# One of five w_gate rows per partition moved to the head of ScalarE's DMA queue, with x behind it

## The chip, the cores and the metric

The kernel runs on one core of one Trainium2 chip. A core has five engines with an instruction queue each: PE (TensorE), DVE (VectorE), ACT (ScalarE), POOL (GpSimd) and SP (SyncE). Transfers between DRAM and on-chip memory are issued from an engine's queue, here from SP and ACT, and carried by 16 DMA engines that all queues share. The metric is the device time of one execution in microseconds (us); less is better.

## What is computed

One decode step for a batch of two tokens with 640 features: layer norm, attention with 32 heads of 192 over the last 2048 positions of a cache of 8192, its output projection and a residual, then layer norm again, a gated feed-forward network of width 1536 and a second residual. Everything stored is bf16.

```
h  = x + A(layernorm(x))                       # x [2, 1, 640]
#    q = xn @ wq [640, 6144]; k, v = the last 2048 of 8192 positions, 32 heads x 192
#    p = softmax(q k^T * 192**-0.5);  A = (p v) @ wo [6144, 640]
n  = layernorm(h)
h2 = h + (gelu(n @ w_gate) * (n @ w_up)) @ w_down   # w_gate, w_up [640, 1536]; w_down [1536, 640]
```

## The kernel before

The work is a single stream of weights and cache through one on-chip buffer, `ring`, of six slots of 24,576 bytes per partition. The 32 heads and two tokens make 16 groups (`NG`), each with one K load and one V load of 3072 KB (24,576 bytes in each of 128 partitions). wq takes 7680 KB, wo comes in four loads of 1920 KB, w_gate is one load of 1920 KB, w_up has two pieces and w_down four (`WUC`, `WDC`, lines 218 and 219). `load` (line 331) puts a transfer on a list, `pump` (line 334) issues it from SP as soon as the loads that lay at its place in the ring were used (`done`, line 349). So all of these go through SP's queue in the order of lines 411 to 422: K0, wq, K1, V0, K2, V1 and so on, then wo, w_gate, w_up, w_down. SP issues a load many microseconds before its bytes move, because earlier loads are still queued.

The one load that SP does not issue is x: line 410 issues it from ACT's queue, ahead of everything else on that engine (line 441, a table load, is next). x is two rows of 1280 bytes. PE's first work is to turn x (`_x_T`, line 466); a layer norm (`layernorm`, line 446) that goes back and forth between DVE, PE and ACT makes xnT from it. Behind the layer norm, in program order on DVE, come the constants (lines 477 to 521), and behind these the copies of K's transposes out of PSUM (line 567).

For each group PE transposes K (`transposes`, line 543), then come scores, softmax, the exponentials' columns and the products with V (`pv`, line 651). `q_rows` (line 569) needs xnT and wq; once it has run, wq's part of the ring is free and SP may issue K2.

The end of the kernel is a chain: `pv(15)`, `o_rows(3)`, `oproj(2)`, `o_columns(3)`, `oproj(3)` (line 696, needs the last wo load), the mean and `h_columns`, hnT (line 779), the w_gate matmuls, the gate's activation, the w_up matmuls, and `uT`, the product of both. The w_down matmuls (line 850) follow in four pieces as their loads land, then one copy (line 856) and the store of the result (line 857).

`ffn_in` (line 792) issues the matmuls of w_gate or w_up. A partition p holds the five rows 5p to 5p+4 of the weight (index c); each c gives four matmuls (line 801) that add into one PSUM bank. Its argument `parts` says which c go together, `loads` which of them came with which load; the instructions of a part wait for hnT and for the load of that part. For w_gate the call is cut in two so that `row_scale` (line 785), the row's normalisation, can go between.

`_Prog` (line 51) keeps the order in which operations are written for each engine, and finds from the names of what they read and write (R, W, X) which semaphores each has to wait for.

Of the kernel before, what the change touches and what calls it, by code (L numbers as in the profile page):

```python
# [5 lines left out]
BF16 = mybir.dt.bfloat16  # L6
# [8 lines left out]
NC5 = D // 128  # L15
# [4 lines left out]
F = 1536  # L20
# [200 lines left out]
K_AT = (0, SLOT, 3 * SLOT, 5 * SLOT)  # L221
# [6 lines left out]
def bass_sequential_preLN__sliding_block_cached__geglu_ffn__decode_kernel(  # L228
# [12 lines left out]
    with ExitStack() as ctx:  # L241

        def sb(name, shape, dt):
            return ctx.enter_context(nc.sbuf_tensor(name, shape, dt))

        def ps(name, shape, dt):
            return ctx.enter_context(nc.psum_tensor(name, shape, dt))
# [29 lines left out]
        ge = sb("ge", [128, 6, 5], F32)  # L277

        xrow = sb("xrow", [128, D], BF16)
        xT = sb("xT", [128, NC5, B], F32)  # L280
        ls = sb("ls", [128, 2, B], F32)
        dT = sb("dT", [128, 2, NC5, B], F32)
# [38 lines left out]
        sps = ps("sps", [128, 512], F32)  # L321
# [4 lines left out]
        P = _Prog()  # L326


        where, live, queue, used = {}, [], [], set()

        def load(key, off, nbytes, src, shape, sem):
            queue.append((key, off, nbytes, src, shape, sem))
# [24 lines left out]
        def load_k(g):  # L357
            load(("k", g), K_AT[g % 4], SLOT, kv_src(A_k_cache, g), lambda v: v, f"k{g % 4}")
# [14 lines left out]
        def wo_parts(J):  # L373
            return ((0, 12),)

        def load_ffn():
            load(("wg", 0), K_AT[1], 2 * NC5 * F, B_w_gate.rearrange("(p c) f -> p c f", c=NC5),
                 lambda v: v.rearrange("p (c f) -> p c f", f=F), "wg")
            for i, (c0, c1) in enumerate(WUC):
                load(("wu", i), K_AT[3] + 2 * c0 * F, 2 * (c1 - c0) * F, B_w_up.rearrange("(p c) f -> p c f", c=NC5)[:, c0:c1, :],  # L380
                     lambda v: v.rearrange("p (c f) -> p c f", f=F), f"wu{i}")
            wd = B_w_down.rearrange("(q p s) n -> q p s n", p=128, s=6)
            for i, (f0, f1) in enumerate(WDC):
                q = f0 // 6
                load(("wd", i), WD_AT[i], 2 * (f1 - f0) * D, wd[q][:, f0 - 6 * q:f1 - 6 * q, :],
                     lambda v: v.rearrange("p (s n) -> p s n", n=D), f"wd{i}")


        def dve(fn, R=(), W=(), X=(), cls=1):
            return P.op("dve", fn, R, W, X, cls=cls)  # L390
# [4 lines left out]
        def pe(fn, R=(), W=(), X=()):  # L395
            return P.op("pe", fn, R, W, X)
# [4 lines left out]
        def ts(out, in0, s1, op0, s2=None, op1=None):  # L401
            def fn(e):
                kw_ = {"op1": op1} if op1 is not None else {}
                return e.tensor_scalar(out=out, in0=in0, scalar1=s1, scalar2=s2, op0=op0, **kw_)  # L404
            return fn

        def tt(out, a, b, op):
            return lambda e: e.tensor_tensor(out=out, in0=a, in1=b, op=op)  # L408

        P.op("act", lambda e: e.dma_start(xrow[0:2, :], A_x[:, 0, :]), W=["xrow"], dma="dx")  # L410
        load_k(0)
        load_wq()
# [7 lines left out]
        load_wo(2)  # L420
        load_wo(3)
        load_ffn()
        pump()

# [360 lines left out]
        def row_scale():  # L785
            pe(lambda e: e.matmul(tps[2][0:98, 0:1], lhsT=lsx[:, :, :].rearrange("p r x -> p (r x)")[:, 0:98], rhs=onesd[:, 0:1],  # L786
                                  start=True, stop=True), R=["lsx", "onesd"], X=[("t", 2)])
            act(lambda e: e.activation(out=lnv[0:98, :], in_=tps[2][0:98, 0:1], func=ACT.Ln, bias=eps_t[0:98, :], scale=1.0),  # L788
                R=["eps"], W=["lnv"], X=[("t", 2)])
            act(lambda e: e.activation(out=rstd[0:98, :], in_=lnv[0:98, :], func=ACT.Exp, scale=-0.5), R=["lnv"], W=["rstd"])  # L790

        def ffn_in(bank, xt, key, parts, loads):
            for c0, c1 in parts:
                i = max(k for k, q in enumerate(loads) if q[0] <= c0)
                wv, wtoks = where[key, i]

                def fn(e, c0=c0, c1=c1, wv=wv, l0=loads[i][0]):
                    for c in range(c0, c1):
                        for r in range(4):
                            cols = wv[:, c - l0, 768 * (r // 2):768 * (r // 2 + 1)].rearrange("p (x s) -> p x s", s=6)  # L800
                            ins = e.matmul(bank[32 * r:32 * r + 2, 0:384], lhsT=hnT[:, c, :], rhs=cols[:, :, 3 * (r % 2):3 * (r % 2) + 3],
                                           start=(c == 0), stop=(c == NC5 - 1), tile_position=(0, 32 * r))
                    return ins

                pe(fn, R=["hnT"] + wtoks, X=[xt])
# [16 lines left out]
        def rjb(t):  # L822
            return t.rearrange("p (r j b) -> p r j b", r=4, j=3)

        ffn_in(sps, "s", "wg", ((0, 2),), ((0, NC5),))
        row_scale()
        ffn_in(sps, "s", "wg", ((2, NC5),), ((0, NC5),))
        dve(ts(grow[0:98, 0:384], sps[0:98, 0:384], rstd[0:98, 0:1], ALU.mult), R=["rstd"], W=["sm"], X=["s"])
        pe(h_rows, R=["hrow", ("hsel", 0), ("hsel", 1)], X=["m1"])
        gT = ffn_columns(grow, ["sm"], tps[0], 0)  # L830
# [10 lines left out]
            W=[("osb", 0), ("osb", 1)], X=["o"])  # L841
        vT = ffn_columns(urow, [("osb", 0), ("osb", 1)], tps[1], 1)
        dve(tt(uT[:, :, 0:17:16].rearrange("p (r j) b -> p r j b", r=4), vT, rjb(ga[:, 0, :]), ALU.mult), R=["ga0"], W=["uT"], X=[("t", 1)])
        for i, (f0, f1) in enumerate(WDC):
            wd, wtoks = where["wd", i]

            def fn(e, f0=f0, f1=f1, wd=wd):
# [10 lines left out]
             dma="dout")  # L858
# [43 lines left out]
```

## Time and profile before

| what | value |
|---|---|
| median of 3 runs | 293.38 us (293.36 to 293.39) |
| the profiled execution | 293.39 us |
| its span, first to last instruction | 291.9 us |
| outside the span | 1.49 us |
| mean granted TensorE clock | 0.842 |
| PE, DVE, ACT busy | 67%, 44%, 33% of the span |
| moved by DMA | 122.44 MB, 419 GB/s over the span |
| w_gate, issue to landing | 1920 KB, 32.4 us |
| a K load, a V load, issue to landing | 31.8 us, 27.7 us (medians) |

Busy shares are averages over stages with different limits. A busy PE need not be what the time hangs on; the chain of waits, followed back from the last instruction, says what was waited for. "PEld" is PE's weight load, "SPq" and "ACTq" stand for the issuing of a transfer in those engines' queues. In the line of 40 slices each digit is a busy share in tenths. Times in the timeline are in us from the start of the span: start, duration, engine, line, what is written from what, how many, and in brackets how long the engine was idle before and what ended that.

### The profile page before, as it was taken

Reading aid. Unit: us, or ns where it says so; the run is one execution under the profiler, and the core shown is the slowest. Engines: PE = TensorE matmul, PEld = TensorE weight load, DVE = VectorE, ACT = ScalarE, POOL = GpSimd, SP = SyncE. Lnnn points to the kernel's source line nnn. Section 1 sums busy time; section 2 is a strip of 40 time slices with the busy share of each in tenths; the row PEclk is TensorE's granted clock in tenths of the full one; section 3 lists DMA queues with packets and bytes.
Section 4 is the critical chain, followed back from the end, with each engine's and each line's share of the span. In section 5 each row is a group of like instructions: output and inputs, shape, how many; then the busy total and the mean of one; then the engine's idle time right before and its main releaser. Section 6 shows DMA issues by size and latency. Waiting matters only on the chain.

```text
span 291.9 us, 5055 instructions
## 1 busy us (share of the span) xinstructions
PE 195.0 (67%) x2141; PEld 151.1 (52%) x2141; DVE 128.4 (44%) x311; ACT 96.1 (33%) x120; POOL 8.6 (3%) x36
## 2 busy tenths in 40 slices
PE   2450768858579197849494597658596858585784
PEld 1450445837376184629282585456575656553341
DVE  5950085434336263616264155426267426262231
ACT  2150125533333152616152154325254325251001
POOL 4000020000000000000000000000000000000000
PEclk9995799797959689977988599979689979796557
DMA  7998999999999999999999999999999999999994
GB/s 290 428 498 362 433 431 430 434 430 431 427 416 445 428 431 429 431 431 431 431 411 442 431 431 428 431 431 428 431 428 428 431 431 428 431 431 426 425 414 174
DMA packets 6362, 122.44 MB, mean 419 GB/s; under 512 B 718, under 2 KB 848, under 8 KB 1360
## 3 DMA queue, kind: packets, MB, share of 16 engines
q1 hardware_dynamic: 6348, 122.30, 98.1%
q8 instruction: 7, 0.11, 0.2%
q14 instruction: 3, 0.02, 0.0%
q10 hardware_dynamic: 4, 0.00, 0.0%
HBM read 122.29 MB, written 0.00 MB: 419 GB/s over the span
## 4 chain that ended last, share of the span: by engine, by line
DMA 76%; PE 19%; SPq 2%; DVE 1%; ACT 1%; issue 0%
DMA ring<-in_A_k_cache_dram 57%; PE tps L555 15%; DMA ring<-in_A_wq_dram 10%; DMA ring<-in_B_w_down_dram 10%; SPq L347 2%; PE tps L576 2%; PE ops L657 1%; ACT ktr L564 1%; PE m L708 1%; PE m L690 1%; DVE ering L408 0%; PE m L850 0%; DVE ktr L567 0%; PE m L641 0%; PE m L671 0%
## 5 line engine op out<-in xcount | busy, mean ns | idle before, releaser
L555 PE MATMUL tps<-identf,ring 128*128 128x128 f32 x768 | 114.4, 317 | 47.6 <-DMA ring<-in_A_k_cache_dram 46.6
L555 PEld LDWEIGHTS tps<-identf,ring 128*128 128x128 f32 x768 | 105.7, 166 | 50.9 <-DMA ring<-in_A_k_cache_dram 48.0
L564 ACT ACTIVATE ktr<-tps 128x1024 bf16<-128x1024 bf16 x80 | 79.3, 1023 | 86.3 <-PE tps L555 86.2
L567 DVE COPY ktr<-tps 128x1024 bf16<-128x1024 bf16 x112 | 74.2, 688 | 74.3 <-PE tps L555 73.6
L632 ACT ACTIVATE eexp<-sm,nm 128x512 bf16<-128x512 f32 x16 | 11.5, 721 | 63.0 <-DVE nm L630 63.0
L657 PE MATMUL ops<-ring,ering 128*32 128x384 bf16 x512 | 25.0, 339 | 3.5 <-DMA ring<-in_A_v_cache_dram 3.4
L621 DVE CUSTOM_DVE_ANT_1 sm<-sps,mska 128x512 f32<-128x512 f32 x16 | 11.1, 691 | 33.7 <-PE sps L613 33.7
L613 PE MATMUL sps<-ktr,rq 128*16 128x512 bf16 x384 | 24.6, 389 | 1.1 <-POOL rq L408 1.1
L657 PEld LDWEIGHTS ops<-ring,ering 128*32 128x32 bf16 x512 | 12.7, 99 | 12.3 <-DMA ring<-in_A_v_cache_dram 5.4
L613 PEld LDWEIGHTS sps<-ktr,rq 128*16 128x16 bf16 x384 | 9.3, 88 | 11.3 <-POOL rq L408 1.2
L628 PEld LDWEIGHTS m<-mrhs,pm 128*128 128x128 bf16 x16 | 1.5, 96 | 23.4 <-DVE mrhs L404 23.4
L628 PE MATMUL m<-mrhs,pm 128*128 128x16 bf16 x16 | 2.9, 183 | 15.7 <-DVE mrhs L404 15.7
L576 PE MATMUL tps<-ring,xnT 128*32 128x384 bf16 x80 | 4.8, 412 | 10.8 <-DMA ring<-in_A_wq_dram 10.8
L408 POOL TENSOR_TENSOR rq<-qs,mask 128x96 bf16<-128x96 bf16 x16 | 5.6, 359 | 194.6 <-PE sps L613 161.5
L576 PEld LDWEIGHTS tps<-ring,xnT 128*32 128x32 bf16 x80 | 2.7, 119 | 12.7 <-issue 11.0
L599 DVE CAST qs<-ops 128x384 bf16<-128x384 f32 x1 | 0.6, 558 | 16.6 <-PE ops L594 16.6
L408 DVE TENSOR_TENSOR ering<-m,mask 128x256 bf16<-128x256 f32 x16 | 6.7, 418 | 2.4 <-PE m L641 2.3
L708 PE MATMUL m<-ring,ot 128*2 128x320 bf16 x96 | 5.5, 382 | 1.6 <-DMA ring<-in_A_wo_dram 1.6
L788 ACT ACTIVATE lnv<-tps,eps_t 98x1 f32<-98x1 f32 x1 | 0.3, 261 | 17.2 <-PE tps L786 17.2
L583 ACT ACTIVATE qrow<-tps 128x768 bf16<-128x768 f32 x1 | 0.8, 810 | 14.6 <-PE tps L576 14.6
L641 PE MATMUL m<-sel,eexp 128*128 128x64 bf16 x64 | 4.8, 200 | 1.2 <-ACT eexp L632 1.2
L408 DVE TENSOR_TENSOR orow<-m,wm 128x1536 bf16<-128x1536 f32 x3 | 5.3, 1751 | 0.0
(124 smaller groups left out, 88.1 us busy)
## 6 DMA issues: line engine op xcount, KB each, us to landing
ring<-in_A_k_cache_dram SPq DMA_DIRECT2D x16, 3072.0 KB, 31.8
ring<-in_A_v_cache_dram SPq DMA_DIRECT2D x16, 3072.0 KB, 27.7
ring<-in_A_wq_dram SPq DMA_DIRECT2D x1, 7680.0 KB, 28.2
ring<-in_A_wo_dram SPq DMA_DIRECT2D x4, 1920.0 KB, 21.8
ring<-in_B_w_gate_dram SPq DMA_DIRECT2D x1, 1920.0 KB, 32.4
ring<-in_B_w_up_dram SPq DMA_DIRECT2D x1, 1536.0 KB, 24.7
ring<-in_B_w_down_dram SPq DMA_DIRECT2D x1, 960.0 KB, 27.2
ring<-in_B_w_down_dram SPq DMA_DIRECT2D x1, 480.0 KB, 27.9
```

Of the source, the lines that this page charges most:

```text
L347: P.op("sp", lambda e, v=v, src=src: e.dma_start(v, src), W=toks + [("sem", sem)], dma=sem)
L408: return lambda e: e.tensor_tensor(out=out, in0=a, in1=b, op=op)
L555: ins = e.transpose(tps[bi][:, 128 * u:128 * (u + 1)], kv[:, off:off + 128], identf[:, :])
L564: act(lambda e, dst=dst, bv=bv: e.activation(out=dst, in_=bv, func=ACT.Copy), W=[("kt", n)], X=[("t", bi)])
L567: dve(lambda e, dst=dst, bv=bv: e.tensor_copy(dst, bv), W=[("kt", n)], X=[("t", bi)], cls=0)
L576: ins = e.matmul(tps[0][32 * r:32 * (r + 1), 0:384], lhsT=xnT[:, c, 32 * J:32 * (J + 1)], rhs=wq[:, c, 1536 * J + 384 * r:1536 * J + 384 * ...
L613: ins = e.matmul(sps[32 * ch:32 * ch + 16, :], lhsT=rq[:, g % 4, k, :], rhs=ktr[:, k // 2, 1024 * ch + k % 2:1024 * (ch + 1):2], start=(k ...
L621: dve(lambda e: e.tensor_tensor_reduce(out=sm[:, :].rearrange("p (u x) -> p u x", u=4), in0=sps[:, :].rearrange("p (u x) -> p u x", u=4), ...
L632: act(lambda e: e.activation(out=eexp[:, :], in_=sm[:, :], func=ACT.Exp, bias=nm[:, 0:1], scale=1.0, accum_out=zr[:, g % 4:g % 4 + 1]), R= ...
L641: ins = e.matmul(o, lhsT=eexp[:, 128 * u:128 * (u + 1)], rhs=sel64[:, :], start=True, stop=True)
L657: ins = e.matmul(ops_[32 * r:32 * (r + 1), 0:384], lhsT=ering[:, g % 4, t, :], rhs=vv[:, 384 * t:384 * (t + 1)], start=(g % 4 == 0 and t < 4),
L708: ins = e.matmul(m1[32 * r:32 * r + 2, 192:512], lhsT=ot[:, kk, :], rhs=wo[:, kk - k0, 320 * h:320 * (h + 1)], start=(kk == 1 or J < 2 and ...
```

## The change

A buffer `wgh` of 3072 bytes per partition is added. A new function `load_wg0` loads row c = 0 of w_gate's five into it, 384 KB in 128 pieces of 3072 bytes, from ACT's queue; it is called before the line that loads x, so x is now the second entry of that queue. The load of w_gate in the ring keeps its place in SP's order and its start in the ring, and carries the other four rows, 1536 KB in pieces of 12,288 bytes where there were 1920 KB in pieces of 15,360. The calls of `ffn_in` for w_gate name two loads; the first call has two parts where it had one. The matmuls and their order are the same.

```
+        wgh = sb("wgh", [128, 1, F], BF16)
...
+        def load_wg0():
+            where["wg", 0] = wgh[:, :, :], ["wgh"]
+            P.op("act", lambda e: e.dma_start(wgh[:, 0, :], B_w_gate.rearrange("(p c) f -> p c f", c=NC5)[:, 0, :]), W=["wgh"], dma="wg0")
+
         def load_ffn():
-            load(("wg", 0), K_AT[1], 2 * NC5 * F, B_w_gate.rearrange("(p c) f -> p c f", c=NC5),
-                 lambda v: v.rearrange("p (c f) -> p c f", f=F), "wg")
+            load(("wg", 1), K_AT[1], 2 * (NC5 - 1) * F, B_w_gate.rearrange("(p c) f -> p c f", c=NC5)[:, 1:NC5, :],
+                 lambda v: v.rearrange("p (c f) -> p c f", f=F), "wg1")
...
+        load_wg0()
         P.op("act", lambda e: e.dma_start(xrow[0:2, :], A_x[:, 0, :]), W=["xrow"], dma="dx")
         load_k(0)
...
-        ffn_in(sps, "s", "wg", ((0, 2),), ((0, NC5),))
+        ffn_in(sps, "s", "wg", ((0, 1), (1, 2)), ((0, 1), (1, NC5)))
         row_scale()
-        ffn_in(sps, "s", "wg", ((2, NC5),), ((0, NC5),))
+        ffn_in(sps, "s", "wg", ((2, NC5),), ((0, 1), (1, NC5)))
```

## The prediction

> **What bounds the kernel.** I read the slices, the queues, the chain of waits, and then the timeline at both ends. From the page:
>
> ```profile
> DMA  7998999999999999999999999999999999999994
> ...
> q1 hardware_dynamic: 6348, 122.30, 98.1%
> q8 instruction: 7, 0.11, 0.2%
> q14 instruction: 3, 0.02, 0.0%
> ```
>
> SP's queue (q1) keeps the 16 DMA engines busy for 98.1% of the span; only the edges are empty. The trace's packet records (start, duration, bytes, queue) sharpen this. q1's first packets start at 2.2 us on eight engines and at 2.5 to 2.7 on the other eight, and the last w_down piece lands at 289.43. Between, an engine goes from piece to piece without gaps: 24,576 bytes in 0.912 us, 15,360 in 0.573, 12,288 in 0.460, 3072 in 0.121. The chain in order of time, at its two ends:
>
> ```profile
> 1.46 28.21 DMA ring<-in_A_wq_dram
> ...
> 260.82 28.19 DMA ring<-in_B_w_down_dram
> 289.01 0.04 issue
> 289.05 0.74 PE m L850 x12
> 289.79 0.02 issue
> 289.81 0.32 DVE yrow L856
> ```
>
> The end waits for the stream's last bytes; behind them lie 0.34 us of matmul latency, the copy and the store. So the time is: start of the stream, its bytes at the engines' rate, and this tail. It is no use to make anything earlier that does not shorten one of the three.
>
> **The end, where the change's matmuls are.** The timeline:
>
> ```profile
> 275.63 1.77 PE L708 MATMUL m<-ring,ot 128*2 128x320 bf16 x24 [1.59 <-DMA ring<-in_A_wo_dram]
> ...
> 279.87 0.17 DVE L408 TENSOR_TENSOR hnT<-m,mean 128x10 bf16<-128x10 f32 x1 [1.08 <-PE m L727]
> ...
> 280.18 0.81 PE L801 MATMUL sps<-ring,hnT 128*2 128x384 bf16 x8 [0.36 <-DVE dT L408]
> ...
> 287.18 0.59 PE L850 MATMUL m<-ring,uT 128*17 128x160 bf16 x24 [0.36 <-DVE uT L408]
> 288.25 0.39 PE L850 MATMUL m<-ring,uT 128*17 128x160 bf16 x12 [0.47 <-DMA ring<-in_B_w_down_dram]
> ```
>
> The reader is to see a chain that starts when the last wo load lands (275.51 in the records of landings, matmuls at 275.63), runs without a real stop to the first w_down matmul at 287.18, and only there waits for DMA again. w_gate's load lands at 280.07, just as hnT is written (280.04).
>
> **The change, part by part.** *Bytes.* They are the same in sum. 8 pieces per engine of 3072 bytes go to the front and 8 of 15,360 become 12,288: 8 x (0.121 + 0.460 - 0.573) = +0.06 us per engine. Everything from K0 to the last wo load is later by 8 x 0.121 = 0.97 us, w_gate and all behind it by 0.06.
>
> *The early row.* Row 0 no longer waits for w_gate's load. hnT comes 0.97 later, at 281.01, and the other four rows land at 280.13: there is no wait to save. Nothing gained.
>
> *The chain at the end.* It starts 0.97 later: 276.60, plus 11.55 (287.18 - 275.63), puts the first w_down matmul at 288.15. The 48 w_down matmuls follow at 17.5 ns (24 weight loads took 0.42), so the last four could start 44 x 17.5 = 0.77 later, at 288.92. Their load lands at 289.43 + 0.06 = 289.49. The chain keeps 0.57 us of slack, and costs nothing as long as that holds; the waits before the second, third and fourth piece give way. The added part of `ffn_in` brings one wait on a semaphore set long before; its price is between nothing and the 0.20 us that PE idles for "issue" between matmul groups here, inside the slack.
>
> *ACT's queue.* One issue more. x's took 0.54 us, SP's of 128 pieces 0.54 to 0.66. The table load behind it moves from 1.30 to about 1.95 and ends near 3.2; ACT's next work is at 6.70. Hidden, with 3.5 us of cover. SP's and POOL's queues keep their order; nothing is moved past them but the transfer itself.
>
> *x behind the row.* Before, x landed at 2.08, and its matmuls waited for DVE's constants:
>
> ```profile
> 0.73 0.54 ACTq L410 DMA_DIRECT2D xrow<-in_A_x_dram  x1
> ...
> 3.75 0.35 PE L468 MATMUL m<-identb,xrow 2*128 2x2 bf16 x5 [3.75 <-DVE eps_t L439]
> ...
> 14.34 1.27 DVE L567 COPY ktr<-tps 128x1024 bf16<-128x1024 bf16 x2
> 15.07 3.72 PEld L555 LDWEIGHTS tps<-identf,ring 128*128 128x128 f32 x32 [0.83 <-DVE ktr L567]
> ```
>
> If an engine takes one piece from each queue in turn, x waits for 8 gate pieces and 8 of K0: 2.2 + 8 x (0.121 + 0.912) + 0.48 (how much longer K0's first pieces took than 0.912, summed per engine) = 10.9; with one wq piece (61,440 bytes, 2.27) in between 13.2. What is queued behind it: on PE the layer norm and K0's transposes; on DVE the layer norm, the constants, and the copies that empty the transposes' banks. From x's matmuls at 3.75 to the end of the transposes at 19.03 are 15.3 us, so with x at 13.2 they end at 28.5. `q_rows` waits for wq, before 29.67, now 30.64. Hidden, with 2.1 us left. If that cover goes, SP issues K2 later than 34.65; its bytes are due at 42.7 (when the first engines end V0) + 0.97, an issue precedes them by 1.46 (K0: 0.74 to 2.2), which makes 7.6 us of cover more.
>
> *Two queues at once.* No row shows two data queues sharing an engine. The nearest rows are the instruction fetches on q8 and q14, each one piece between two of q1 on one engine. Three of 8 KB took 0.31 to 0.32 and lengthened q1's next piece by 0.38 to 0.66, 0.84 in all on average; six of 16 KB took 0.98 to 1.11 and lengthened it by 0.47 to 0.55, 1.55 in all. A line through both gives 0.13 us per turn beside the bytes; the lengthening alone, taken as the price of a turn, gives 0.5. Over 8 turns that is 1.04 or 4.0 us lost. On the other side, x's packets moved at 1.67, 0.53 before K0's, and K0's first pieces lost 0.48 us: a second queue could use both, and at best its whole 0.97 is hidden. I take nothing, near the middle of these bounds: between two loads of one queue the records show no loss at all, and what the fetches cost grows with their bytes, as a slow target would make it.
>
> The Trainium skill ("DMA: Bandwidth & Descriptors", section "Issuing engines are not separate DMA queues") says that loads issued by different engines run on the same 16 DMA engines and interleave, and that issuing from several only saves the sequencer's time. By that rule the gain of 0.97 is out; no run here shows it so far.
>
> Sum, against the profiled execution: 293.39 + 0.06 = 293.45, rounded with the small unknown of the added wait to 293.5. That execution is 0.01 above the median.
>
> **Rivals.** *The early row is hidden in the start (faster).* For: 0.53 us of empty engines and 0.48 us of slow pieces. Against: all 16 engines slow down together until 4.0 to 4.5 us, as by something that they share, which a second queue would share too. Time: 293.45 - 0.97 = 292.5; the chain at the end then starts as before, and could start the last four matmuls at 287.18 + 0.77 = 287.95, ahead of their load at 288.5.
>
> *Each turn between the queues costs (slower).* Place: K0's eight pieces on every engine, 2 to 11 us. Price: 8 x 0.13 gives 294.5, 8 x 0.5 gives 297.4. It decides from 0.07 us a turn, which makes 0.59. For: the fetches. Against: their dependence on bytes.
>
> *The chain at the end becomes the bound.* If the clock, granted at 1.0 from 285.24 to 288.65 and at 0.5 before and after, does not rise, the 44 matmuls take 0.77 more and the transposes before them 0.2: 0.97 - 0.57 = 0.4 over, 293.9. Against: the work that went before the rise is only shifted.
>
> *x waits for whole loads.* If an engine finishes K0 and then wq before it turns to ACT's second load, x lands at about 29.5, the transposes end at 44.8, `q_rows` (4.83) at 49.6, and K2's bytes come at 51.1, where they were due at 43.7: 7.4 us of empty engines, 300.8. It decides from x at 22. Against: fetches got in between pieces of one load, one after three of wq's eight.
>
> The Trainium skill (the same page, "Queues, rings and completion order") has a DMA engine take turns between queues by packets of typically 9 to 17 descriptors. If a packet held all eight pieces of a load, that would be this last rival; the fetch inside wq speaks against it.
>
> **How the numbers follow.** Forecast 0.32, hidden 0.25, turns 0.30, chain 0.07, x late 0.06. About 0.2% (0.59 us) is what a measurement of this kernel can tell from no change. Faster is the hidden row, 0.25. Within are the forecast and the chain, 0.39. Slower are the turns and the late x, 0.36. The range goes from 292.5 (most of the hidden cases) to 294.7 (the turns at 0.13); the dearer turns and the late x stay out. The forecast's own range, with partial hiding and the chain, is 293.0 to 293.9.
>
> **What would show it.** Right: in the packet records K0's pieces at 0.912 between the gate's at 0.121; wq landing at 30.6; x's matmuls at 11 to 13 and no wait of `q_rows` other than for wq; the last wo load landing near 276.5, the last w_down piece at 289.5 with the copy right behind. Longer K0 pieces mean turns that cost; wq landing at 29.7 means a hidden row; w_down matmuls that wait for uT alone mean the chain; a DMA share below 9 near 44 us a late x. The forecast is wrong if wq lands outside 30.2 to 31.0.

## The result and the profile after

| | before | changed |
|---|---|---|
| median (22 runs each) | 293.32 us (293.13 to 293.72) | 292.94 us (292.74 to 293.27) |
| ratio, 95% interval | | 0.9987 (0.9981 to 0.9993) |
| span of the profiled execution | 291.9 us | 291.4 us |

The change makes the kernel 0.38 us faster. The forecast was 293.5, no change; the range 292.5 to 294.7 holds the time, the sign is wrong. Two more sets of the changed kernel, each beside its own runs of the kernel before, gave 0.9991 (0.9983 to 1.0) and 0.999 (0.9981 to 0.9999).

The page of the changed kernel, slices and queues:

```profile
span 291.4 us, 5056 instructions
...
DMA  8999999999999999999999999999999999999994
...
q1 hardware_dynamic: 6348, 121.90, 97.8%
q10 hardware_dynamic: 148, 0.40, 0.5%
```

The stream still fills the span. What changed is the first digit, 8 where there was 7, and ACT's queue, q10, which now carries the row. The start in windows of half a microsecond (window, its length, busy time and count of PE, PEld, DVE, ACT, POOL, granted clock, DMA share, GB/s), first before:

```profile
1.50:2.00 0.50, 0.00 (x0) 0.00 (x0) 0.44 (x3) 0.50 (x1) 0.50 (x3) 1.00 0.02 5
2.00:2.50 0.50, 0.00 (x0) 0.00 (x0) 0.50 (x1) 0.50 (x1) 0.50 (x1) 1.00 1.01 393
```

and the changed kernel:

```profile
1.50:2.00 0.50, 0.00 (x0) 0.00 (x0) 0.44 (x3) 0.06 (x1) 0.50 (x3) 1.00 1.09 104
2.00:2.50 0.50, 0.00 (x0) 0.00 (x0) 0.50 (x1) 0.50 (x1) 0.50 (x1) 1.00 0.38 86
2.50:3.00 0.50, 0.00 (x0) 0.00 (x0) 0.50 (x1) 0.50 (x1) 0.50 (x1) 1.00 0.91 362
```

A window counts a packet where it starts; long packets make the single shares jump. What can be read is where traffic begins: half a microsecond earlier. The packet records have it exactly. Before, the first pieces start between 2.18 and 2.28 us on eight engines and by 2.66 on all 16. Now the row's start at 1.74, by 1.97 on 15 engines and at 2.30 on the last. The row's eight pieces per engine are done by 3.07 to 3.5, and K0's begin right behind.

| | before | changed | expected |
|---|---|---|---|
| how much longer than usual the first pieces took, per engine | K0: 0.48 us | the row 0.51, K0 0.03 | K0: 0.48 |
| wq landed | 29.67 | 30.07 | 30.64 |
| last wo load landed | 275.49 | 275.89 | 276.46 |
| last w_down piece landed | 289.40 | 288.90 | 289.46 |

Everything up to w_gate is 0.40 us later, not 0.97; everything behind it is 0.50 earlier, not 0.06 later. Both say that 0.56 to 0.57 us of the row's transfer cost nothing. The two ends of the chain of waits after, as shown of before:

```profile
1.46 28.61 DMA ring<-in_A_wq_dram
...
261.19 27.31 DMA ring<-in_B_w_down_dram
288.50 0.04 issue
288.55 0.74 PE m L856 x12
289.29 0.02 issue
289.31 0.33 DVE yrow L862
```

It is the same chain, with the same tail behind the last bytes: the copy starts at 289.31 in place of 289.81. The timeline at the start:

```profile
0.73 0.38 ACTq L379 DMA_DIRECT2D wgh<-in_B_w_gate_dram  x1
0.74 0.66 SPq L348 DMA_DIRECT2D ring<-in_A_k_cache_dram  x1
...
1.15 0.76 ACTq L416 DMA_DIRECT2D xrow<-in_A_x_dram  x1
...
5.81 0.33 PE L474 MATMUL m<-identb,xrow 2*128 2x2 bf16 x5 [5.81 <-DMA xrow<-in_A_x_dram]
...
17.10 5.45 PE L561 MATMUL tps<-identf,ring 128*128 128x128 f32 x32 [2.15 <-DVE ktr L573]
```

The row takes 0.38 us to issue, K0 0.66. x now is what PE waits for first, until 5.81 in place of 3.75, and K0's transposes end at 22.55 in place of 19.03. wq lands at 30.07, so this is hidden, with 7.5 us to spare.

### The profile page after: what moved, and what is told of

It is laid out like the page before. It is cut to its first block, busy times and chain, and to the rows that moved or that the text cites. A ratio compares the mean times of both kernels' runs of the same rounds, so it can differ in the third digit from the quotient of the medians.

```text
span 291.4 us, 5056 instructions
## 1 busy us (share of the span) xinstructions
PE 194.3 (67%) x2141; PEld 150.9 (52%) x2141; DVE 128.6 (44%) x311; ACT 96.0 (33%) x120; POOL 8.6 (3%) x36
## 4 chain that ended last, share of the span: by engine, by line
DMA 76%; PE 19%; SPq 2%; DVE 1%; issue 0%
DMA ring<-in_A_k_cache_dram 57%; PE tps L561 15%; DMA ring<-in_A_wq_dram 10%; DMA ring<-in_B_w_down_dram 9%; PE tps L582 2%; SPq L348 2%; PE ops L663 1%; PE m L714 1%; PE m L696 1%; DVE ktr L573 0%; DVE ering L413 0%; PE m L856 0%; PE m L647 0%; PE m L677 0%; DVE yrow L862 0%
## 5 line engine op out<-in xcount | busy, mean ns | idle before, releaser
L619 PEld LDWEIGHTS sps<-ktr,rq 128*16 128x16 bf16 x384 | 9.2, 88 | 11.4 <-POOL rq L413 1.2
L582 PE MATMUL tps<-ring,xnT 128*32 128x384 bf16 x80 | 5.5, 455 | 7.7 <-DMA ring<-in_A_wq_dram 7.7
L714 PE MATMUL m<-ring,ot 128*2 128x320 bf16 x96 | 4.1, 307 | 2.5 <-DMA ring<-in_A_wo_dram 2.5
L673 DVE COPY osb<-ops 128x192 f32<-128x192 f32 x8 | 2.5, 353 | 6.0 <-PE ops L663 6.0
```

Source lines behind the costliest of these rows:

```text
L582: ins = e.matmul(tps[0][32 * r:32 * (r + 1), 0:384], lhsT=xnT[:, c, 32 * J:32 * (J + 1)], rhs=wq[:, c, 1536 * J + 384 * r:1536 * J + 384 * ...
L619: ins = e.matmul(sps[32 * ch:32 * ch + 16, :], lhsT=rq[:, g % 4, k, :], rhs=ktr[:, k // 2, 1024 * ch + k % 2:1024 * (ch + 1):2], start=(k ...
L714: ins = e.matmul(m1[32 * r:32 * r + 2, 192:512], lhsT=ot[:, kk, :], rhs=wo[:, kk - k0, 320 * h:320 * (h + 1)], start=(kk == 1 or J < 2 and ...
```

## The experiments

Two explanations stood: the stream starts earlier because of what goes first (the early start), or the row that is already there helps at the end of the kernel. Within the first it was open whether the second queue, the shape of the load, or these very bytes matter. All ratios are to the kernel before on the same chip.

**The row first in SP's queue.** The second queue is taken away, the row and its place ahead of K0 stay.

```
-            P.op("act", lambda e: e.dma_start(wgh[:, 0, :], ...), W=["wgh"], dma="wg0")
+            P.op("sp", lambda e: e.dma_start(wgh[:, 0, :], ...), W=["wgh"], dma="wg0")
```

> The gate row is the first load of SP's queue, ahead of K0; ACT's queue holds x alone. Early start by a load that is quick to set up (issue 0.38 us against K0's 0.66): first packets at about 1.7 to 1.8 us, wq lands near 30.05 as in the changed kernel (29.67 before), time 292.9 to 293.0. Early start by a second queue working beside SP: packets not before 2.2, nothing hidden, wq lands near 30.6, time 293.4. Gain at the end of the kernel from the row that is already there: 292.95 either way.

Measured: packets at 1.75, wq landed at 30.17, the last w_down piece at 289.03. In the profile this is the early start, without a second queue:

```profile
0.74 0.39 SPq L379 DMA_DIRECT2D wgh<-in_B_w_gate_dram  x1
1.19 0.64 SPq L348 DMA_DIRECT2D ring<-in_A_k_cache_dram  x1
```

The profiled execution took 292.93, but the median is 293.4, ratio 1.0014 (0.9998 to 1.0031), with single runs up to 295.45. The same kernel once more:

> The gate row first in SP's queue once more. Early start by a plain pattern: as the changed kernel, 292.95; if the wide spread of its first runs (292.93 to 295.45) comes from SP issuing the row and K0 one after the other: again spread, median 293.3 to 293.5.

Median 293.45, 1.0004 (0.9995 to 1.0013), single runs from 292.99 to 294.61. This time a long execution was profiled (294.43): the row again starts at 1.75, and 14 engines begin K0 between 2.99 and 3.51. Two engines stand idle when their part of the row is done, and get their first piece of K0 only at 4.91 and 4.95. Two engines end wq 2 us behind the others (31.63 and 31.67, against 29.67 for the ninth of 16), and the last w_down piece lands at 290.16. So the early start needs no second queue, but with row and K0 in one queue it is lost again in most runs. Why two engines get K0 so late there is open; K0's issue ran from 1.19 to 1.83 in both profiles of this kernel, and in the first no engine stood idle.

**The row issued later from ACT, and x first.** Two kernels with the changed kernel's end but without the early start: the row behind x and the table load, or right behind x.

```
-        load_wg0()
         P.op("act", lambda e: e.dma_start(xrow[0:2, :], A_x[:, 0, :]), W=["xrow"], dma="dx")
+        load_wg0()      # x first; in the other kernel this stands behind the table load
```

> The gate row is issued from ACT behind x and the table load, at about 2.6 us, so its bytes come when SP's queue already keeps the engines busy. Early start: nothing is hidden, wq lands near 30.6, the last w_down piece at 289.5, time 293.4. Gain at the end of the kernel: still 292.95. A price per turn between two queues: K0's rows show more than the 0.48 us per engine over 0.912 that they show before, and the time is 294.5 at 0.13 us a turn, 297.4 at 0.5.

> x is the first load of ACT's queue again, the gate row the second, issued some 0.54 us later. Early start: the row's packets come at about 2.2 to 2.3 us, when K0's come too; at most 0.1 us hidden, wq near 30.5, time 293.3 to 293.4, x lands at 2.05. Gain at the end of the kernel: 292.95.

Measured: 293.7 both, ratios 1.0007 (0.9998 to 1.0016) and 1.001 (1.0001 to 1.0019). The help at the end is out: the same end is no faster here than before. The two kernels hardly differ: the row's issue begins at 1.34 behind the table load (2.6 was expected) and at 1.30 with x first. In both the row's pieces start at 4.5 to 4.6, not at 2.3, when the engines have done about two pieces of K0 each; then they go about one for one between K0's until 11.4. Nothing is hidden: wq lands at 30.78 and 30.64. K0's pieces take 0.64 and 0.68 us per engine longer than usual against 0.48: eight turns cost 0.16 to 0.20, some 0.02 us each. With x first the last w_down piece lands at 289.46, which is the 0.06 of the forecast's bytes. Yet the time is 0.3 longer than before. The end of that kernel:

```profile
276.58 1.77 PE L714 MATMUL m<-ring,ot 128*2 128x320 bf16 x24 [2.34 <-DMA ring<-in_A_wo_dram]
...
288.28 1.45 PEld L856 LDWEIGHTS m<-ring,uT 128*17 128x17 bf16 x48 [0.61 <-DVE uT L413]
288.28 1.78 PE L856 MATMUL m<-ring,uT 128*17 128x160 bf16 x48 [0.31 <-DVE uT L413]
290.11 0.33 DVE L862 CAST yrow<-m 113x160 bf16<-113x160 f32 x1 [1.89 <-PE m L856]
```

All 48 w_down matmuls stand in one group behind uT, without a wait for DMA between them: here the chain sets the end. Its matmuls take 1.78 us, because the clock is at half. The window in question before, and then with x first:

```profile
287.00:288.00 1.00, 0.59 (x24) 0.42 (x24) 0.08 (x1) 0.00 (x0) 0.00 (x0) 1.00 0.54 211
```

```profile
288.00:289.00 1.00, 0.72 (x24) 0.72 (x28) 0.22 (x1) 0.00 (x0) 0.00 (x0) 0.50 0.34 128
```

The third number from the right is the granted clock: 1.00 before, 0.50 here. At 1.0, 24 weight loads took 0.42 us, 17.5 ns each; at 0.5, all 48 took 1.45, 30 ns each. The forecast took the matmuls at the full clock, and so saw 0.57 us of slack that is not there.

In the changed kernel the clock is at 0.5 here too, and it escapes only just. Its chain starts 0.40 later than before, but the 24 matmuls of `oproj(3)` took 1.16 us (1.77 before and with x first), because the granted clock was 1.00 from 275.6 to 276.6 (0.50 before), so the first w_down matmul comes at 287.10 and the last ones still wait for DMA. In another execution of the changed kernel, the one profiled for after_third, those 24 matmuls took 1.64 us, and the chain itself sets the end, by an estimated 0.1 us: the last piece landed at 288.99, and 0.41 later, as in the first, would be 289.40. One line of the first, then two of the second:

```profile
288.94 0.10 PEld L856 LDWEIGHTS m<-ring,uT 128*17 128x17 bf16 x4 [0.28 <-DMA ring<-in_B_w_down_dram]
```

```profile
287.67 1.78 PE L856 MATMUL m<-ring,uT 128*17 128x160 bf16 x48 [0.31 <-DVE uT L413]
289.50 0.32 DVE L862 CAST yrow<-m 113x160 bf16<-113x160 f32 x1 [1.89 <-PE m L856]
```

So the changed kernel has next to no slack at its end.

**K0's own first bytes from ACT.** Does it matter what goes first? w_gate stays whole; ACT's first load is the start of K0.

```
+            P.op("act", lambda e: e.dma_start(ring[:, K_AT[0] // 2:(K_AT[0] + cut) // 2], kv_src(A_k_cache, 0)[:, :, 0:cut // 2]), W=toks, dma="k0h")
             ...
+            load(("k", 0), K_AT[0] + cut, SLOT - cut, src0[:, :, cut // 2:], lambda v: v, "k0")      # cut = 3072
```

> The kernel before, with w_gate whole and in its place; the first 3072 bytes per partition of K0 are the first load of ACT's queue, the other 21,504 stay SP's first load. Early start: it does not matter which bytes go first; packets at about 1.75 us, wq lands near 29.1 (29.67 before), the last w_down piece near 288.9, time 292.8 to 293.0. Gain at the end of the kernel from the gate row: none is there, 293.3.

Measured: 293.8, ratio 1.0014 (1.0005 to 1.0023), a miss; wq landed at 29.82. The pieces are as many and as long as the row's (128 of 3072 bytes), in the same queue and place, but the load takes 0.63 us to issue and its packets start at 2.15:

```profile
0.73 0.63 ACTq L364 DMA_DIRECT2D ring<-in_A_k_cache_dram  x1
0.74 0.66 SPq L347 DMA_DIRECT2D ring<-in_A_k_cache_dram  x1
```

That explains why nothing is gained. Of the 0.41 us that the median loses, the profiled execution (293.69) shows the stream's end 0.16 later, at 289.56; the rest is open.

Together with the row on SP this is a table of two by two:

| first packet, us | issued by ACT | issued by SP |
|---|---|---|
| w_gate's row, one even stride over 128 partitions | 1.74 (changed kernel) | 1.75 (row_sp) |
| K0's pattern, four heads of 32 partitions | 2.15 (k0_split) | 2.18 (before) |

When the first packet moves is decided by the pattern, not by the queue. Why the nested pattern is later no run shows: its issue takes some 0.25 us longer, its first packet comes 0.4 us later.

**K0 by heads.** If K0's pattern is slow to set up, four loads with a plain pattern each should start early.

```
+            for h in range(4):
+                src = A_k_cache[0, h, SKT - WIN:, :].rearrange("(i t) d -> i (t d)", t=TPG)
+                P.op("sp", lambda e, h=h, src=src: e.dma_start(ring[32 * h:32 * (h + 1), ...], src), W=[("k0h", h)], dma=f"k0h{h}")
```

> The kernel before, with K0 loaded by four loads of one head each (32 partitions by 24,576 bytes) on SP's queue in place of one over four heads; all bytes and their order stay. Early start by a load that is quick to set up: packets at 1.7 to 1.8 us in place of 2.2, wq lands near 29.2 (29.67 before), the last w_down piece near 288.9, time 292.8 to 292.9. If a second queue or the small rows make the early start: packets at 2.2, time 293.4.

Measured: 300.76, ratio 1.0254 (1.024 to 1.0267). The start came as expected, packets at 1.76; what followed did not. Of this kernel, windows of 3 us:

```profile
5.00:8.00 3.00, 0.74 (x3) 0.57 (x3) 1.39 (x10) 0.47 (x2) 0.00 (x0) 1.00 1.24 254
8.00:11.00 3.00, 0.00 (x0) 0.00 (x0) 2.79 (x19) 0.00 (x0) 0.00 (x0) 1.00 0.79 172
```

The last column is what to read: 254 and 172 GB/s, where the stream has some 430 in nearly all slices of the page. While K0 came in, a piece of 24,576 bytes took 1.91 us where it takes 0.912 when all 128 partitions are written at once. K0's last pieces ended at 17.3 in place of 10.6, wq landed 7.3 us later, at 36.98, and the end is later by as much.

**Two rows.** Is every early byte hidden, or only what fits into the earlier start?

```
-        wgh = sb("wgh", [128, 1, F], BF16)
+        wgh = sb("wgh", [128, 2, F], BF16)      # and rows 0 and 1 in the load, 2 to 4 in the ring
```

> Two of w_gate's five rows are the first load of ACT's queue (768 KB, 6144 bytes per partition). The start hides no more than with one row (about 0.57 us per engine), so the last wo load lands near 276.9 (275.49 before, 275.89 with one row). If the chain behind it sets the end then: first w_down matmul at 288.0 to 288.6, no wait of the w_down matmuls for DMA, time 293.5 to 294.0. If the stream's end alone counts: 292.95. If every early row is hidden: 292.4.

Measured: 293.95, ratio 1.0019 (1.001 to 1.0028); the profiled execution was one of the fastest, 293.37. In it the last wo load landed at 276.89, as expected; the last w_down piece at 289.03, which is no earlier than with one row. The second row is paid in full in the front, and the w_down matmuls (287.95, 1.78 us for all 48) run without a wait. The chain sets the end. Its `oproj(3)` matmuls took 0.99 us there; at the 1.77 of the kernel before, the end would come 0.78 later, which is an estimate and would fit the executions of 293.85 to 294.27. None of those was profiled.

**64 KB first.** The first pieces of the stream are slow whatever they are. Can a small load take that on itself?

```
+        wgp = sb("wgp", [128, 256], BF16)
...
+        P.op("act", lambda e: e.dma_start(wgp[:, :], B_w_gate.rearrange("(p c) f -> p c f", c=NC5)[:, 0, 0:256]), W=["wgp"], dma="wgp")
```

> The kernel before, with 64 KB (512 bytes per partition, used for nothing) as the first load of ACT's queue, x behind it. If the slow first pieces belong to whatever moves first: packets at 1.75, K0's pieces show under 0.2 us per engine over 0.912 in place of 0.48, time 293.1. If they belong to K0's load: still 0.48, time 293.4.

Measured: 293.75, ratio 1.0014 (1.0005 to 1.0022). Packets at 1.75, and K0's first pieces took 0.60 us per engine longer than usual: not less. The slowness belongs to the first large pieces (K0 0.48 before, the row 0.51 in the changed kernel, K0's start 0.60 in k0_split). It moved, and no run shows it gone. The profiled execution took 293.4, the stream's end came no later than before (289.32); why most executions are longer is open. One of the 12 executions took 580.03 us, which no profile explains; it is not in the ratio, and without it the median is 293.66.

**wq's first bytes.** A plain pattern, no byte of w_gate, and nothing moved from the end of the kernel to the front.

```
+            P.op("act", lambda e: e.dma_start(ring[:, WQ_AT // 2:(WQ_AT + HEAD) // 2], A_wq.rearrange("(p c) n -> p (c n)", c=NC5)[:, 0:HEAD // 2]),
+                 W=toks, dma="wqh")      # HEAD = 3072
...
+            load("wq", WQ_AT + HEAD, 2 * NC5 * HQ * DH - HEAD, A_wq.rearrange("(p c) n -> p (c n)", c=NC5)[:, HEAD // 2:],
+                 lambda v: v, "wq")
```

> The kernel before; the first 3072 bytes per partition of wq, a plain pattern like the gate row's, are the first load of ACT's queue with x behind it, K0 and the rest of wq are SP's first two; w_gate is whole and in its place. Early start by a plain pattern: packets at 1.75 us, the bytes keep their order behind wq, so wq lands near 29.1, the last wo load near 274.9 (275.49 before, 275.89 with the gate row), the last w_down piece near 288.85; the chain at the end keeps its slack and the w_down matmuls wait for DMA; time 292.8. If the gain needed w_gate's row: 293.4.

> The changed kernel on the chip of these runs, a third set of it beside the kernel before: 292.9 to 293.05.

Measured: 293.06, ratio 0.9991 (0.9982 to 0.9999); the changed kernel beside it 293.08, 0.999 (0.9981 to 0.9999). Packets at 1.74, wq landed at 29.17, the last wo load at 275.00, the last w_down piece at 288.92. The end of the kernel with wq's head:

```profile
286.69 0.59 PE L864 MATMUL m<-ring,uT 128*17 128x160 bf16 x24 [0.54 <-DMA ring<-in_B_w_down_dram]
287.76 0.58 PE L864 MATMUL m<-ring,uT 128*17 128x160 bf16 x12 [0.48 <-DMA ring<-in_B_w_down_dram]
288.57 0.71 PE L864 MATMUL m<-ring,uT 128*17 128x160 bf16 x12 [0.22 <-DMA ring<-in_B_w_down_dram]
```

The whole gain of the changed kernel is there without w_gate's row, with a chain that waits for DMA three times and so has slack. The time expected was 0.26 too low: in the profiled execution, the fastest of the eleven at 292.83, the stream's end came 0.48 earlier; the median is only 0.32 lower. This kernel and the changed one are equal; none of the versions beats the changed kernel.

**More of wq.** The same with HEAD = 12288.

> The same with 12,288 bytes per partition of wq. The early start does not grow with the bytes: the same 292.8, K0 lands some 3 us later without cost. If more bytes hide more: 292.0 or less.

Measured: 302.09. The time tells nothing of the question, because the head then fills the whole part of wq that shares a ring slot with K2, so nothing in the ring's bookkeeping kept K2 back: K2 is loaded over wq's head before `q_rows` reads it, part of q is computed from K2's bytes, and `q_rows` waits until K2 has landed. SP's queue of that kernel:

```profile
9.49 0.54 SPq L348 DMA_DIRECT2D ring<-in_A_k_cache_dram  x1
56.53 0.54 SPq L348 DMA_DIRECT2D ring<-in_A_v_cache_dram  x1
```

K2 was issued at 9.49 and the load after it only at 56.53, and the engines ran dry between. What lies ahead of this does answer the question: wq landed at 29.22, against 29.17 with 3072 bytes in front, and K0 at 14.10, against 11.22. More bytes in front hid no more.

The second set of the changed kernel, beside the kernels with two rows, K0 by heads and 64 KB:

> The changed kernel once more, on the chip of the others: 292.9 to 293.0, 0.4 us under the kernel before.

Measured: 293.04.

## Why the prediction was wrong

- *What bounds the kernel* was right. The profiled executions follow from the start of the stream, its bytes and the tail, except where the chain at the end took over and where K2, issued too early, left the engines empty (wq_head4). The medians of row_sp, prime and rows2 lie 0.35 to 0.58 above their profiled executions; only for row_sp was a longer execution profiled too.
- *Two queues at once* is the step that failed. It bounded the effect of the row in front between a gain of 0.97 and a loss of 4.0, and put nothing for it in the sum, as the middle of the bounds. Measured, 0.57 us are hidden; with that term the sum is 293.45 - 0.57 = 292.88, and the profiled execution took 293.00. The text had the row for it: x's packets moved at 1.67, 0.53 us before K0's. It read this as a property of a second queue and set it against the fetches' price. The two by two table shows a property of the load: one with a plain pattern gets its first packets 0.4 us sooner than K0's, from either queue. The time that an engine has no piece up to 4.0 us and what its first pieces take too long, summed, fell from 2.94 us per engine to 2.41 (2.40 and 2.44 in the two other profiles of the changed kernel). That is nearly the whole 0.57.
- *The fetches as the nearest rows for a turn* misled: 0.02 us a turn (row_late, x_first) lies below the 0.13 and 0.5 that they gave. The rival built on them is out.
- *x waits for whole loads*: the Trainium skill ("DMA: Bandwidth & Descriptors", "Queues, rings and completion order") lets an engine change queues by packets of several descriptors. With the row issued late the pieces went about one for one, so here a turn was a single piece, and in the changed kernel x came after one piece of K0. The rival is out.
- *The rival of the hidden row* was half right. Of its two parts the 0.53 us of empty engines was there to be had; the 0.48 us of slow first pieces was not, as the text argued against it.
- *The Trainium skill's rule* ("DMA: Bandwidth & Descriptors", "Issuing engines are not separate DMA queues"), that issuing from several engines only saves the sequencer's time, agrees with the runs: the row starts as early from SP, 1.75, as from ACT, 1.74. Yet the choice of queue was not free of effect here: with both loads on SP the median was 293.4 and 293.45, without the gain. The gain that the text ruled out by that rule came from another cause, on which that section is silent.
- *The chain at the end*: its length to the first w_down matmul was about right (11.55 us; 11.70 with x first, and 11.07, 11.28 and 11.57 in the three profiles of the changed kernel, whose `oproj(3)` matmuls took 1.16, 1.36 and 1.64 us); the slack of 0.57 was not there. The 48 matmuls took 1.78 us at half clock, where 0.77 and a latency of 0.34 were put. (The text reads the last landing of the kernel before as 289.43; the record of landings has 289.40, which alone makes the slack 0.54.) With the 0.97 us of the forecast the chain does set the end, 0.3 us late (x_first, 293.7), so the rival of the chain was right in its mechanism (it said 293.9). The changed kernel has its stream only 0.40 later there; even so the chain set its end in one of three profiles.
- *The early row* saves no wait: right, by the two kernels that have it without the early start.
- *x*: the forecast had it land at 10.9 to 13.2; it landed at 5.67, after a single piece of K0. That it is hidden was right.

## What to carry to other kernels

In a kernel bound by one stream of transfers, look at when its first packet moves, and at the pattern of the load that goes first: a load with a single even stride over all partitions, put in front of one with a nested pattern and issued from another queue, fills the time before the other's first packet; from the same queue the gain was lost in most executions here. Only as much as fits into that time is gained; more bytes in front only push what lies behind them, and a chain that hangs on a load in the middle may then become the bound. Take the slack of such a chain at the lower of the clocks that the profile shows.

## What the runs showed of the hardware that was not expected

- The first packet of a load of 128 pieces of 3072 bytes that was the first of its queue came 1.0 us after its issue began with w_gate's even stride, 1.4 with K0's four heads of 32 partitions. The same row issued 0.6 us later, with K0 already on its way, got its first packet 3.2 to 3.3 us after its issue began, behind two pieces of K0 per engine.
- Loads of 24,576 bytes into 32 partitions at a time ran at less than half the rate: 1.91 us a piece against 0.912 for 128 partitions (k0_heads).
- The first large pieces of the stream together took 0.36 to 0.70 us per engine longer than usual where no second load came between them, also behind a load of 64 KB that came first (0.60); in the long execution of the kernel with row and K0 on SP it was 0.97.
- Two data queues taking turns on an engine cost some 0.02 us a turn; an instruction fetch of 16 KB, in the kernel before, cost 1.5 us on its engine (1.0 for itself, 0.5 on the next piece).
